# Moving the statistics of eight token tiles from VectorE to ScalarE, and splitting four operand sums in two

## The chip, the cores and the metric

One core of a Trainium2 chip. The metric is the device time of one execution in microseconds (us), the median of several runs. All matrix products are float32 values split into a high and a low part (fp32r), each product being three matmuls: high times high, high times low, low times high.

## The reference

```
x  = A_x                                    # 2048 tokens x 512
xn = (x - mean(x)) / sqrt(var(x) + 1e-5)    # per token
a  = xn @ dft_hid_re.T;  b = xn @ dft_hid_im.T
y  = dft_seq_re @ a - dft_seq_im @ b        # 2048 x 512
h  = gelu(xn @ w_gate) * (xn @ w_up)        # 512 -> 1792
out = x + y + h @ w_down
```

## The kernel before

x is held as 16 token tiles `xs[n]` of 128 tokens x 512 values. Each tile is normalised in place: mean and variance into the columns of one small tile `stats` (`ln_stats`: `bn_stats`, then `bn_aggr`, on VectorE), an approximate reciprocal root on ScalarE (`ln_root`), four small VectorE instructions that refine it (`ln_refine`), and one ScalarE activation with a scale and a bias column (`ln_affine`, L1304, "apply"). Then ScalarE rounds the tile to its high part (`split_hi`, L251) and VectorE subtracts to get the low part (`split_lo`, L256).

The sequence transform comes first, in four chunks of 512 columns. In chunk 0, token tiles 0 to 3 and 8 to 11 are multiplied plainly (the z matmuls, operands `pan`, `xa`, `xb`, `xf`). Tiles 4 to 7 (the set `J`) are paired with tiles 12 to 15, and each pair goes through a seven-product scheme of Strassen's kind (the m matmuls, operands `ps` and `xa`, `xf`, `xc`). In the later chunks all eight pairs do. A step of pass 0 of a pair multiplies products 0, 5, 6 and 4, a step of pass 1 products 1, 3 and 2; every product is 2 column halves x 3 matmuls. The x operands of products 4, 5, 6 and 2 are sums of quarters of the two tiles: `sum_of(k, 0..3)` forms four 128x256 sums on VectorE (L1364 to L1371); the sums for products 4 and 5 share one 128x512 tile, those for 6 and 2 another. `sum_hi` rounds such a tile on ScalarE in one instruction (`xch`), and `split_lo` gives its low part on VectorE (`xcl`). After the last pair of a pass the products are combined (L1440 to L1452) in the PSUM banks in which pass 1 goes on. The combined results of two chunks are multiplied with the hidden-dimension matrices (the y matmuls, operands z and d). After that come the two gated layers (a, b, c, dn matmuls).

The order of the instructions of chunks 0 and 1 is not written by hand. A planner (`Plan`) is given every operation with its engine, its cost in us, what it comes after and which buffers it uses. TensorE's order is fixed; the time at which TensorE would reach each product gives every other operation its due time. The planner then walks through time and gives each engine, among the operations that can start, the one that can start first, and among those the one due first; the list that results is the order of instructions on each engine. Nothing is reordered at run time. Loads go through SP's queue and stores to DRAM through POOL's, in the planner's order too. The engine names in the planner are p (TensorE), v (VectorE), a (ScalarE), s (SP), g (POOL). Costs that matter here: V5 .6, V2 .333, V1 .1 (VectorE: 512 columns, 256 columns, tiny), A5 .52, A2 .31 (ScalarE: 512 and 256 columns).

`group(ns)` enters the normalisation of one or two tiles; the groups are [2], [3], [8, 9], [10, 11] and the four pairs (4, 12), (5, 13), (6, 14), (7, 15). Tiles 0 and 1 are handled ahead of the planner.

Of the kernel before, what the change touches and what calls it, by code (L numbers as in the profile page):

```python
# [9 lines left out]
F32R = mybir.dt.float32r  # L10
BF16 = mybir.dt.bfloat16
AF = mybir.ActivationFunctionType
OP = mybir.AluOpType

P = 128
S = 2048
D = 512
# [8 lines left out]
HD = D // 2  # L26
HS = NS // 2
WARM = 9
WARM_END = 3
SLOTS = 109  # L30
J = (4, 5, 6, 7)
NP = NF
EPS = 1e-5

# [183 lines left out]
def fnet_geglu_kernel(ctx: ExitStack, tc: tile.TileContext, x, xt, cs, dh, wgu, wd, out):  # L218
# [7 lines left out]
    nc = tc.nc  # L226
# [8 lines left out]
    def slot(name, dtype=F32, shape=(P, D)):  # L235
        return mem.tile(list(shape), dtype, name=name, tag="mem")
# [13 lines left out]
    def split_hi(t, src, sign=1):  # L250
        nc.scalar.activation(t[0], src, AF.Copy, scale=float(sign))  # L251

    def split_lo(t, src, sign=1, engine=nc.vector):
        hi = t[0].bitcast(F32)
        if sign > 0:
            engine.tensor_sub(t[1], src, hi)  # L256
        else:
            engine.scalar_tensor_tensor(t[1], src, -1.0, hi, op0=OP.mult, op1=OP.subtract)
# [30 lines left out]
    stats = const.tile([P, 2, NS], F32, name="stats")  # L289
    ident = const.tile([P, P], F32, name="ident")  # L290
    eps = const.tile([P, 1], F32, name="eps")
# [10 lines left out]
    xs, ln, xn = {}, {}, {}  # L302
# [14 lines left out]
    def ln_stats(ns):  # L317

        ops = []
        for n in ns:  # L320
            parts = 1 if n else 2
            bn = small.tile([P, parts, 6], F32, name="bn")
            for h in range(parts):
                ops.append(lambda h=h, n=n, bn=bn, whole=parts == 1: nc.vector.bn_stats(
                    bn[:, h], xs[n] if whole else xs[n][:, h * HD:(h + 1) * HD]))
            ops.append(lambda n=n, bn=bn: nc.vector.bn_aggr(stats[:, :, n], bn))
        for i in range(2, len(ops) - 1, 2):
            if len(ns) > 1:
                ops[i - 1], ops[i] = ops[i], ops[i - 1]
        return ops  # L330

    def ln_root(ns):
        w = small.tile([P, 9], F32, name="w")
        var = stats[:, 1, span(ns)]
        nc.scalar.activation(w[:, :len(ns)], var, AF.Abs_reciprocal_sqrt, bias=eps)
        for n in ns:
            ln[n] = w

# [11 lines left out]
    def ln_refine(ns):  # L350
        k = len(ns)
        w = ln[ns[0]]
        r, t, b = (w[:, i * 3:i * 3 + k] for i in range(3))
        mean, var = (stats[:, i, span(ns)] for i in range(2))

        return [lambda a=a: nc.vector.scalar_tensor_tensor(*a[:4], op0=a[4], op1=OP.mult) for a in (
            (t, var, EPS, r, OP.add), (t, t, -0.5, r, OP.mult), (var, t, 1.5, r, OP.add), (b, mean, -1.0, var, OP.mult))]

    def ln_apply(ns, early=False):
        for i, n in enumerate(ns):  # L360
            src, kw = xs[n], dict(scale=stats[:, 1, n:n + 1], bias=ln[n][:, 6 + i:7 + i])
            his = []
            if n not in xn:
                if n < HS:
                    xn[n] = [hl_half(f"x{'ab'[h]}{n}") for h in range(1 if n in J else 2)]
                    his = [(xn[n][h][0], src[:, h * HD:(h + 1) * HD]) for h in range(len(xn[n]))]
# [17 lines left out]
    full = {}  # L384
    PL = [n for n in range(NS) if n % HS not in J]
    XO = PL + [n + h for n in J for h in (0, HS)]

# [97 lines left out]
    xc, xsum = {}, []  # L485
# [372 lines left out]
    def load_wd(q):  # L858

        if q < NP:  # L860
            wx["d", q] = [slot("wd", F32, (P, 2, HD)) for _ in range(2)]
# [11 lines left out]
    hs, hl, acc = {}, {}, {}  # L873
# [328 lines left out]
    warm = const.tile([P, CH], BF16, name="warm")  # L1202
# [42 lines left out]
        begin_products(k, slice(a, a + 1))  # L1245

    L = len(seq)
    V5, V2, V1, A5, A2, MB = .6, .333, .1, .52, .31, .262
    plan = Plan(dict(p=10.9, v=12.0, a=11.7, s=5.6, g=8.0), 18, SLOTS - 2, AHEAD)
    plan.dma, land = 12.8, 8.75  # L1250
# [18 lines left out]
    for n in range(2):  # L1269
        plan.done(("apply", n), 11.)  # L1270
        for h in range(2):
            plan.done(("xlo", n, h), 12.)
            plan.size["xn", n, h] = 1

    def group(ns):
        ops = ln_stats(ns)
        names, todo = [], [(n, f) for n in ns for f in ("bn", "ag")]
        if len(ns) > 1:
            for i in range(2, len(todo) - 1, 2):
                todo[i - 1], todo[i] = todo[i], todo[i - 1]  # L1280
        for (n, f), op in zip(todo, ops):
            plan.add((f, n), "v", .58 if f == "bn" else V1, op, after=[("x", n) if f == "bn" else ("bn", n)], uses=[("xs", n)])
        key = ns[0]
        plan.add(("root", key), "a", .2, lambda: ln_root(ns), after=[("ag", n) for n in ns])
        box = []

        def refine(i):
            if not box:
                box.extend(ln_refine(ns))
            box[i]()  # L1290
        for i in range(4):
            plan.add(("ref", key, i), "v", V1, lambda i=i: refine(i), after=[("ref", key, i - 1) if i else ("root", key)])
        for i, n in enumerate(ns):
            plan.add(("apply", n), "a", .72, lambda i=i, n=n: ln_affine(n, i), after=[("ref", key, 3)], uses=[("xs", n)])
            parts = 1 if n >= HS or n in J else 2
            for h in range(parts):
                wide = n >= HS
                plan.add(("xhi", n, h), "a", A5 if wide else A2, lambda n=n, h=h: x_hi(n, h), after=[("apply", n)],
                         uses=[("xs", n)], makes={("xn", n, h): 2 if wide else 1})
                plan.add(("xlo", n, h), "v", V5 if wide else V2, lambda n=n, h=h: x_lo(n, h), after=[("xhi", n, h)],  # L1300
                         uses=[("xs", n), ("xn", n, h)])
# [22 lines left out]
    def x_part(n, h):  # L1324
        return ("xlo", n, 0) if n >= HS else ("xlo", n, h)
# [16 lines left out]
    for k in range(2, L):  # L1342
        n, m = seq[k]
        for d in range(ND):
            xu = ("xn", n, d // 2 if n < HS else 0)
            plan.add(("pe", k, d), "p", 3 * MM, lambda k=k, d=d: plain_product(k, d), after=[("plo", k), x_part(n, d // 2)],
                     uses=[("ph", k)] + ([xu] if n < HS and d > 1 else []), holds=[("z", m, d)])
# [3 lines left out]
    st = {}  # L1351

    def sum_hi(k, r, t):
        hl = slot("xch", F32R, (P, 2, HD)), slot("xcl", F32R, (P, 2, HD))
        for i in range(2):
            xc[r[i], k] = hl[0][:, i], hl[1][:, i]
        split_hi(hl, t)
        st["hl", k, r[0]] = hl, t

    def sum_of(k, j):  # L1360
        u, v = xs[k], xs[k + HS]
        if j == 0:
            st[k, 0] = slot("xs", F32, (P, 2, HD))
            nc.vector.tensor_add(st[k, 0][:, 0], u[:, HD:], v[:, HD:])  # L1364
        elif j == 1:
            nc.vector.tensor_sub(st[k, 0][:, 1], st[k, 0][:, 0], u[:, :HD])
        elif j == 2:
            st[k, 1] = slot("xs", F32, (P, 2, HD))
            nc.vector.tensor_sub(st[k, 1][:, 0], u[:, :HD], u[:, HD:])
        else:  # L1370
            nc.vector.tensor_sub(st[k, 1][:, 1], v[:, :HD], st[k, 0][:, 1])  # L1371

    for k in range(HS):
        xu = [("xs", k), ("xs", k + HS)]
        both = [("apply", k), ("apply", k + HS)]
        for j, (after, tiles) in enumerate(((both, [("t", k, 0)]), ([("s", k, 0)], [("t", k, 0)]), (both, [("t", k, 1)]),
                                            ([("s", k, 1), ("s", k, 2)], [("t", k, 0), ("t", k, 1)]))):
            plan.add(("s", k, j), "v", V2, lambda k=k, j=j: sum_of(k, j), after=after, uses=xu + tiles[:None if j % 2 else 0],
                     makes={} if j % 2 else {tiles[0]: 1})
        for j, r in enumerate(((4, 5), (6, 2))):  # L1380
            plan.add(("shi", k, j), "a", A5, lambda k=k, j=j, r=r: sum_hi(k, r, st[k, j]), after=[("s", k, 2 * j + 1)],
                     uses=[("t", k, j)], makes={("xc", k, j): 2})
            plan.add(("slo", k, j), "v", V5, lambda k=k, r=r: split_lo(*st["hl", k, r[0]]), after=[("shi", k, j)],
                     uses=[("t", k, j), ("xc", k, j)])

    def operand(c, r, k):
        k = pair(c, k)
        xc[0, k], xc[1, k], xc[3, k] = xn[k][0], xn[k + HS][0], xn[k + HS][1]
        return xc[r, k]

    def operand_ready(c, r, k):
        k = pair(c, k)
        return {0: x_part(k, 0), 1: x_part(k + HS, 0), 3: x_part(k + HS, 1)}.get(r) or ("slo", k, 0 if r in (4, 5) else 1)

    def load_one(i, key):
        c, p, k = steps[i]
# [194 lines left out]
    for r, g in ((0, 0), (0, 1), (1, 0), (1, 1)):  # L1591
        plan.add(("y", r, g), "p", 12 * MM, lambda r=r, g=g: z_y(r, g), uses=[("do", r, g)] + [("z0", (r, g, e)) for e in range(2)],
                 after=[("dlo", r, g), *(("zlo", (r, g, e)) for e in range(2))],
                 banks=[("y", r, j) for j in range(2)] * (g == 0), holds=[("y", r, j) for j in range(2)])
        if g:
            plan.add(("yo", r), "a", 1.04, lambda r=r: y_copy(r), after=[("y", r, g), *([("res", 0, 0)] if r else ["st2"])],
                     makes={("po", r): 2}, holds=[("y", r, j) for j in range(2)])
# [9 lines left out]
    for g in range(2):  # L1607
        t = {(kb, oh): ("d2", g, kb, oh) for kb in range(2) for oh in range(2)}
# [9 lines left out]
    for kb in range(2):  # L1618
        for g in range(2):
            plan.add(("fz", kb, g), "s", .9, lambda kb=kb, g=g: fetch_z(0, kb, g), mb=2 * MB, makes={("zr", kb, g, e): 1 for e in range(2)},  # L1620
                     after=[("dzp", *KT[kb, g], e) for e in range(2)])
# [3 lines left out]
    for r in (4, 2, 6, 5, 3):  # L1625
        both = [("y", 1, r, j) for j in range(2)]
        for g in range(2):
            plan.add(("y", r, g), "p", 12 * MM, lambda r=r, g=g: z_y(r, g), uses=[("do", r, g)] + [("z", (r, g, e)) for e in range(2)],
                     after=[("dlo", r, g), *(("zlo", (r, g, e)) for e in range(2))], banks=both * (g == 0), holds=both)
# [3 lines left out]
    for j in range(4):  # L1633
        i = n1 + j
        c, p, k = steps[i]
# [4 lines left out]
        else:  # L1640
            for key in PANELS[p]:
                plan.add(("ld", i, key), "s", .45, lambda i=i, key=key: load_one(i, key), mb=MB, due=END + 12,
                         makes={("r", i, key): 1})
# [12 lines left out]
    for i, (c, p, k) in enumerate(steps):  # L1656
# [34 lines left out]
        else:  # L1691
            for n, (r, g) in enumerate((r, g) for r in (4, 2, 6, 5, 3)[:5 if c < NC - 1 else 3] for g in range(2)):
# [13 lines left out]
                if n in (2, 4) and c == NC - 1:  # L1706
                    t = n // 2 - 1
# [56 lines left out]
```

## Time and profile before

| | |
|---|---|
| median of 3 runs | 798.88 us (798.71 to 799.8) |
| profiled execution | 799.29 us, of which the profile's span is 797.2 us |
| TensorE busy | 792.6 us (99%) |
| VectorE busy | 722.3 us (91%) |
| ScalarE busy | 505.7 us (63%) |
| POOL busy | 157.2 us (20%) |
| DMA | 177.47 MB, mean 223 GB/s |

The page is of one execution. The span runs from the first to the last instruction; the profiled execution's own time is 2.09 us longer. In the views, PE is TensorE's matmuls, PEld its weight loads, DVE VectorE, ACT ScalarE, SPq the queue of SP. A row of a timeline has start and duration in us, engine, line, operation, output <- inputs with shapes, how many instructions it merges, and in brackets the idle time before it and what ended that. Durations of neighbours on an engine overlap, so the distance from start to start is what an instruction costs.

### The profile page before, as it was taken

To read this page: it belongs to the slowest core of one execution; us is meant where nothing else is said; L and a number is where in the kernel's file an instruction comes from. 1 tells how busy PE (TensorE), PEld (TensorE's weight loads), DVE (VectorE), ACT (ScalarE), POOL (GpSimd) and SP (SyncE) were. 2 spreads that over 40 slices of the span, in tenths; PEclk is the share of its full clock that TensorE was granted. 3 is DMA by queue.
4 is the path that set the end of the run, shared out by engine and by line. 5 is a ranking of instruction groups with operands and counts; after the bars stand their busy time and mean duration, and the time that the engine had idled before them with its cause. 6 is when DMAs were issued, how large, how long until landed. Compare 5 with 4: busy or idle time off the path is not lost.

```text
span 797.2 us, 11453 instructions
## 1 busy us (share of the span) xinstructions
PE 792.6 (99%) x3487; PEld 652.9 (82%) x3487; DVE 722.3 (91%) x1336; ACT 505.7 (63%) x952; POOL 157.2 (20%) x228
## 2 busy tenths in 40 slices
PE   9999999999999999999999999999999999999998
PEld 6888888888888888888888888888888888888886
DVE  7999999989999979899999998898878779989787
ACT  6786555556544555365658866866766677576564
POOL 0000510034211231000203422321222233121100
PEclk9999999999999999999999999999999999999999
DMA  9856898778999887778726987868965799887942
GB/s 334 314 183 199 303 345 256 248 252 256 373 359 331 327 282 290 261 263 302 189 65 139 210 160 167 191 111 212 264 125 97 123 237 152 174 209 139 250 109 106
DMA packets 90477, 177.47 MB, mean 223 GB/s; under 512 B 10832, under 2 KB 14448, under 8 KB 90224
## 3 DMA queue, kind: packets, MB, share of 16 engines
q1 hardware_dynamic: 65328, 118.27, 44.3%
q0 software_dynamic: 24800, 58.21, 34.4%
q8 instruction: 27, 0.44, 0.2%
q14 instruction: 34, 0.28, 0.1%
q10 hardware_dynamic: 288, 0.26, 0.1%
HBM read 114.29 MB, written 65.55 MB: 226 GB/s over the span
## 4 chain that ended last, share of the span: by engine, by line
PE 99%; DVE 0%; issue 0%; ACT 0%; DVEq 0%
PE m L267 33%; PE dn L267 17%; PE b L267 14%; PE c L267 10%; PE a L267 10%; PE y L267 9%; PE z L267 6%; PE warm L1207 1%; DVE dl L256 0%; DVE z411l L256 0%; ACT dh L251 0%; DVE ds L433 0%; DVE p L1002 0%; PE warm L1209 0%; DVE warm L1203 0%
## 5 line engine op out<-in xcount | busy, mean ns | idle before, releaser
L251 ACT ACTIVATE psh<-pan 128x512 fp32r<-128x512 f32 x196 | 112.3, 625 | 74.6 <-DVE pan L644 29.6
L256 DVE TENSOR_TENSOR psl<-pan,psh 128x512 fp32r<-128x512 f32 x196 | 125.9, 681 | 5.4 <-ACT psh L251 4.7
L923 POOL DMA_DIRECT2D partial<-part x94 | 81.0, 868 | 234.9 <-ACT part L922 200.9
L267 PE MATMUL m<-psh,xch 128*128 128x512 f32 x224 | 87.3, 390 | 0.0
L267 PE MATMUL m<-psl,xch 128*128 128x512 f32 x224 | 87.2, 389 | 0.0
L267 PE MATMUL m<-psh,xcl 128*128 128x512 f32 x224 | 87.2, 389 | 0.0
L922 ACT ACTIVATE part<-dn 128x512 f32<-128x512 f32 x94 | 55.4, 605 | 24.5 <-PE dn L267 22.2
L256 DVE TENSOR_TENSOR wl<-ws,wh 128x512 fp32r<-128x512 f32 x84 | 55.0, 683 | 0.3 <-ACT wh L251 0.2
L251 ACT ACTIVATE wh<-ws 128x512 fp32r<-128x512 f32 x84 | 49.6, 629 | 0.8 <-DMA xT_hl<-xT51h 0.7
L267 PEld LDWEIGHTS m<-psh,xch 128*128 128x128 f32 x224 | 42.0, 188 | 9.1 <-DVE m L1452 0.3
L267 PEld LDWEIGHTS m<-psh,xcl 128*128 128x128 f32 x224 | 42.0, 188 | 8.7
L267 PEld LDWEIGHTS m<-psl,xch 128*128 128x128 f32 x224 | 42.1, 188 | 8.7
L1147 ACT ACTIVATE w<-b 128x512 f32<-128x512 f32 x28 | 16.8, 599 | 47.0 <-PE b L267 46.9
L557 POOL DMA_DIRECT2D partial<-part x28 | 20.8, 787 | 106.3 <-ACT part L553 97.5
L1150 DVE TENSOR_TENSOR w<-c,w 128x512 f32<-128x512 f32 x28 | 19.3, 689 | 24.3 <-ACT w L1147 24.3
L256 DVE TENSOR_TENSOR htl<-s,hth 128x512 fp32r<-128x512 f32 x56 | 35.9, 684 | 4.2 <-ACT hth L251 4.1
L267 PE MATMUL m<-psh,xa 128*128 128x512 f32 x112 | 39.0, 389 | 0.0
L895 DVE TENSOR_TENSOR s<-s 128x512 f32<-128x512 f32 x56 | 37.4, 687 | 1.0
L639 DVE TENSOR_TENSOR pan<-pan 128x512 f32<-128x512 f32 x56 | 36.5, 678 | 0.0
L256 DVE TENSOR_TENSOR wl<-wx,wh 128x512 fp32r<-128x512 f32 x28 | 19.2, 686 | 16.2 <-ACT wh L251 16.2
L251 ACT ACTIVATE hth<-s 128x512 fp32r<-128x512 f32 x56 | 32.4, 642 | 1.0 <-DVE s L895 1.0
L267 PE MATMUL dn<-hl,wh 128*128 128x512 f32 x84 | 32.8, 390 | 0.0
(774 smaller groups left out, 2342.6 us busy)
## 6 DMA issues: line engine op xcount, KB each, us to landing
pan<-in_cs SPq DMA_DIRECT2D x156, 256.0 KB, 5.4
partial<-part POOLq DMA_DIRECT2D x122, 256.0 KB, 5.1
wx<-in_wgu SPq DMA_DIRECT2D x56, 256.0 KB, 4.9
t_park<-pan POOLq DMA_DIRECT2D x28, 256.0 KB, 5.0
pan<-t_park SPq DMA_DIRECT2D x28, 256.0 KB, 4.5
wd<-in_wd SPq DMA_DIRECT2D x28, 256.0 KB, 4.3
acc<-partial SPq DMA_DIRECT2D x28, 256.0 KB, 5.3
zr<-z_park SPq DMA_DIRECT2D x16, 256.0 KB, 4.0
```

The lines of the kernel that those rows point to most:

```text
L251: nc.scalar.activation(t[0], src, AF.Copy, scale=float(sign))
L256: engine.tensor_sub(t[1], src, hi)
L267: nc.tensor.matmul(ps, a[u][:, sl], b[v], start=first and r == 0, stop=last and r == 2, skip_group_check=resumed)
L557: nc.gpsimd.dma_start(partial[sp, r, j], ypart.pop((r, j)), **({} if r in (0, 5, 6) else {"accum_op": OP.add}))
L639: return [lambda: nc.vector.tensor_sub(t3, b22, b12), lambda: nc.vector.tensor_sub(t1, b12, b11), lambda: (nc.vector.tensor_sub(b22, b22, ...
L895: nc.vector.tensor_sub(t, u, v)
L922: nc.scalar.activation(t, ps[j], AF.Copy)
L923: nc.gpsimd.dma_start(partial[sp, r, j], t, accum_op=OP.add)
L1147: nc.scalar.activation(w, b, AF.Copy)
L1150: nc.vector.tensor_add(w, c, w)
L1207: nc.tensor.matmul(ps, warm[:, :P], warm, start=i == 0, stop=False)
```

## The change

For the tiles of the four pairs (4 to 7 and 12 to 15) the mean and the variance are computed by ScalarE: a Copy with scale 1/512 whose accumulated output is the mean, then a Square with scale -1 and the mean as its bias column, whose accumulated output is 512 times the variance. The elementwise output goes to the small `warm` tile and is not used. The root and the refinement take the factor 512 into account. In the planner the two are entered under the old names ("bn", n) and ("ag", n), now on engine a with costs 0.72 and 0.82.

For the same pairs the operand tile of products 6 and 2 is rounded and subtracted in two halves of 256 columns: high half and low half for product 6, then for product 2. The sum for product 2 comes after the high half of product 6. Product 2 waits for the second low half alone. `operand` sets the references to x operands one by one, for the product that uses them.

```diff
@@ -29,6 +29,7 @@
 WARM_END = 3
 SLOTS = 109
 J = (4, 5, 6, 7)
+AST = {n + h for n in J for h in (0, HS)}
 NP = NF
 EPS = 1e-5
 
@@ -332,7 +333,7 @@
     def ln_root(ns):
         w = small.tile([P, 9], F32, name="w")
         var = stats[:, 1, span(ns)]
-        nc.scalar.activation(w[:, :len(ns)], var, AF.Abs_reciprocal_sqrt, bias=eps)
+        nc.scalar.activation(w[:, :len(ns)], var, AF.Abs_reciprocal_sqrt, bias=eps, scale=1 / D if ns[0] in AST else 1.0)
         for n in ns:
             ln[n] = w
 
@@ -353,8 +354,9 @@
         r, t, b = (w[:, i * 3:i * 3 + k] for i in range(3))
         mean, var = (stats[:, i, span(ns)] for i in range(2))
 
+        m = D if ns[0] in AST else 1
         return [lambda a=a: nc.vector.scalar_tensor_tensor(*a[:4], op0=a[4], op1=OP.mult) for a in (
-            (t, var, EPS, r, OP.add), (t, t, -0.5, r, OP.mult), (var, t, 1.5, r, OP.add), (b, mean, -1.0, var, OP.mult))]
+            (t, var, EPS * m, r, OP.add), (t, t, -0.5 / m, r, OP.mult), (var, t, 1.5, r, OP.add), (b, mean, -1.0, var, OP.mult))]
 
     def ln_apply(ns, early=False):
         for i, n in enumerate(ns):
@@ -1245,6 +1247,7 @@
         begin_products(k, slice(a, a + 1))
 
     L = len(seq)
+    ASUM = .72
     V5, V2, V1, A5, A2, MB = .6, .333, .1, .52, .31, .262
     plan = Plan(dict(p=10.9, v=12.0, a=11.7, s=5.6, g=8.0), 18, SLOTS - 2, AHEAD)
     plan.dma, land = 12.8, 8.75
@@ -1272,14 +1275,24 @@
             plan.done(("xlo", n, h), 12.)
             plan.size["xn", n, h] = 1
 
+    def act_mean(n):
+        nc.scalar.activation(warm, xs[n], AF.Copy, scale=1 / D, accum_out=stats[:, 0, n:n + 1])
+
+    def act_var(n):
+        nc.scalar.activation(warm, xs[n], AF.Square, scale=-1.0, bias=stats[:, 0, n:n + 1], accum_out=stats[:, 1, n:n + 1])
+
     def group(ns):
-        ops = ln_stats(ns)
-        names, todo = [], [(n, f) for n in ns for f in ("bn", "ag")]
-        if len(ns) > 1:
-            for i in range(2, len(todo) - 1, 2):
-                todo[i - 1], todo[i] = todo[i], todo[i - 1]
-        for (n, f), op in zip(todo, ops):
-            plan.add((f, n), "v", .58 if f == "bn" else V1, op, after=[("x", n) if f == "bn" else ("bn", n)], uses=[("xs", n)])
+        if ns[0] in AST:
+            for n in ns:
+                plan.add(("bn", n), "a", ASUM, lambda n=n: act_mean(n), after=[("x", n)], uses=[("xs", n)])
+                plan.add(("ag", n), "a", ASUM + .1, lambda n=n: act_var(n), after=[("bn", n)], uses=[("xs", n)])
+        else:
+            todo, ops = [(n, f) for n in ns for f in ("bn", "ag")], ln_stats(ns)
+            if len(ns) > 1:
+                for i in range(2, len(todo) - 1, 2):
+                    todo[i - 1], todo[i] = todo[i], todo[i - 1]
+            for (n, f), op in zip(todo, ops):
+                plan.add((f, n), "v", .58 if f == "bn" else V1, op, after=[("x", n) if f == "bn" else ("bn", n)], uses=[("xs", n)])
         key = ns[0]
         plan.add(("root", key), "a", .2, lambda: ln_root(ns), after=[("ag", n) for n in ns])
         box = []
@@ -1357,6 +1370,13 @@
         split_hi(hl, t)
         st["hl", k, r[0]] = hl, t
 
+    def half_hi(k, i):
+        if i == 0:
+            hl = slot("xch", F32R, (P, 2, HD)), slot("xcl", F32R, (P, 2, HD))
+            for e in range(2):
+                xc[(6, 2)[e], k] = hl[0][:, e], hl[1][:, e]
+        split_hi(xc[(6, 2)[i], k], st[k, 1][:, i])
+
     def sum_of(k, j):
         u, v = xs[k], xs[k + HS]
         if j == 0:
@@ -1374,10 +1394,17 @@
         xu = [("xs", k), ("xs", k + HS)]
         both = [("apply", k), ("apply", k + HS)]
         for j, (after, tiles) in enumerate(((both, [("t", k, 0)]), ([("s", k, 0)], [("t", k, 0)]), (both, [("t", k, 1)]),
-                                            ([("s", k, 1), ("s", k, 2)], [("t", k, 0), ("t", k, 1)]))):
+                                            ([("s", k, 1), ("s", k, 2), *[("shi", k, 1)] * (k in J)], [("t", k, 0), ("t", k, 1)]))):
             plan.add(("s", k, j), "v", V2, lambda k=k, j=j: sum_of(k, j), after=after, uses=xu + tiles[:None if j % 2 else 0],
                      makes={} if j % 2 else {tiles[0]: 1})
         for j, r in enumerate(((4, 5), (6, 2))):
+            if j and k in J:
+                for i in range(2):
+                    plan.add(("shi", k, 1 + i), "a", A2, lambda k=k, i=i: half_hi(k, i), after=[("s", k, 2 + i)],
+                             uses=[("t", k, 1), ("xc", k, 1)] if i else [("t", k, 1)], makes={} if i else {("xc", k, 1): 2})
+                    plan.add(("slo", k, 1 + i), "v", V2, lambda k=k, i=i: split_lo(xc[(6, 2)[i], k], st[k, 1][:, i]),
+                             after=[("shi", k, 1 + i)], uses=[("t", k, 1), ("xc", k, 1)])
+                continue
             plan.add(("shi", k, j), "a", A5, lambda k=k, j=j, r=r: sum_hi(k, r, st[k, j]), after=[("s", k, 2 * j + 1)],
                      uses=[("t", k, j)], makes={("xc", k, j): 2})
             plan.add(("slo", k, j), "v", V5, lambda k=k, r=r: split_lo(*st["hl", k, r[0]]), after=[("shi", k, j)],
@@ -1385,12 +1412,14 @@
 
     def operand(c, r, k):
         k = pair(c, k)
-        xc[0, k], xc[1, k], xc[3, k] = xn[k][0], xn[k + HS][0], xn[k + HS][1]
+        for q, n, h in ((0, k, 0), (1, k + HS, 0), (3, k + HS, 1)):
+            if q == r:
+                xc[r, k] = xn[n][h]
         return xc[r, k]
 
     def operand_ready(c, r, k):
         k = pair(c, k)
-        return {0: x_part(k, 0), 1: x_part(k + HS, 0), 3: x_part(k + HS, 1)}.get(r) or ("slo", k, 0 if r in (4, 5) else 1)
+        return {0: x_part(k, 0), 1: x_part(k + HS, 0), 3: x_part(k + HS, 1)}.get(r) or ("slo", k, 0 if r in (4, 5) else 1 + (r == 2 and k in J))
 
     def load_one(i, key):
         c, p, k = steps[i]
```

## Prediction

> **What bounds the kernel now.** I read the page first, for the share of each engine, then TensorE's timeline for its cadence, then the stretches of 10 us, because the edited work lies between 20 and 100 us.
>
> ```profile
> span 797.2 us, 11453 instructions
> PE 792.6 (99%) x3487; PEld 652.9 (82%) x3487; DVE 722.3 (91%) x1336; ACT 505.7 (63%) x952; POOL 157.2 (20%) x228
> ```
>
> A busy PE is not yet a PE at its peak, so the starts of single matmuls decide. These are the first z matmuls after the slow start, the first m matmul of each sequence chunk, and the widest gap between them:
>
> ```profile
> 8.01 0.62 PE L267 MATMUL z<-panh,xa 128*128 128x512 f32 x2
> ...
> 49.73 0.39 PE L267 MATMUL m<-psh,xa 128*128 128x512 f32 x1
> ...
> 98.84 0.39 PE L267 MATMUL m<-psh,xa 128*128 128x512 f32 x1
> ...
> 177.93 0.40 PE L267 MATMUL y<-z410h,dh 128*128 128x512 f32 x1
> 178.46 0.50 PE L267 MATMUL y<-z410h,dl 128*128 128x512 f32 x1
> ...
> 202.99 0.39 PE L267 MATMUL m<-psh,xa 128*128 128x512 f32 x1
> ```
>
> From 8.01 to 49.73 us the code issues 184 z matmuls (16 panels x 4 blocks x 3 terms, less the 8 before 8.01): 41.72 / 184 = 0.2267 us each, with no gap. From 49.73 to 98.84 it issues 4 pairs x 42 + 4 y blocks x 12 = 216: 48.98 us at that rate, and 49.11 passed, so 0.13 is lost. From 98.84 to 202.99 it issues 8 x 42 + 10 x 12 = 456: 103.39 us against 104.15, so 0.76 is lost, 0.30 of it in the one gap at 178 (0.53 between starts). **All that TensorE could win in the part that the planner orders is 0.13 + 0.76 = 0.9 us, 0.11% of the time.** The number of matmuls doesn't change.
>
> ```profile
> 20.00:30.00 10.00, 10.00 (x45) 8.26 (x45) 10.00 (x30) 5.53 (x12) 0.00 (x0) 1.00 1.04 379
> 30.00:40.00 10.00, 10.00 (x46) 8.27 (x45) 10.00 (x26) 8.84 (x18) 0.72 (x1) 1.00 0.70 248
> 40.00:50.00 10.00, 10.00 (x46) 8.29 (x45) 9.81 (x27) 9.00 (x18) 0.56 (x1) 1.00 0.53 177
> 50.00:60.00 10.00, 10.00 (x46) 8.29 (x45) 10.00 (x25) 8.55 (x16) 1.05 (x2) 1.00 0.56 184
> 60.00:70.00 10.00, 10.00 (x46) 8.29 (x45) 9.81 (x19) 8.70 (x17) 0.03 (x1) 1.00 0.67 210
> 70.00:80.00 10.00, 10.00 (x46) 8.29 (x45) 10.00 (x18) 5.11 (x9) 0.00 (x0) 1.00 0.55 187
> ```
>
> The columns after the stretch's length are PE, PEld, DVE, ACT and POOL, busy time each. VectorE is full, but it runs ahead of TensorE: a full engine that nobody waits for. ScalarE has 4.47 + 1.16 + 1.00 + 1.45 + 1.30 = 9.4 us free from 20 to 70 us, and 4.9 in the ten after. The granted clock is 1.00 throughout.
>
> **VectorE's side of the change.**
>
> ```profile
> 51.04 1.28 DVE L324 BATCH_NORM_STATS2 bn<-x 128x6 f32<-128x512 f32 x2
> 52.23 0.41 DVE L1364 TENSOR_TENSOR xs<-x,x 128x256 f32<-128x256 f32 x1
> 52.56 0.42 DVE L256 TENSOR_TENSOR xa<-x,xa 128x256 fp32r<-128x256 f32 x1
> ...
> 56.31 0.24 DVE L326 BATCH_NORM_AGGREGATE stats<-bn 128x2 f32<-128x6 f32 x2
> 56.47 0.66 DVE L639 TENSOR_TENSOR pan<-pan 128x512 f32<-128x512 f32 x1
> ```
>
> What an operation costs its engine is the distance to the next start. Two statistics take 52.23 - 51.04 = 1.19, two aggregates 0.16; eight tiles take 8 x (0.60 + 0.08) = 5.4 us, which go. The low parts of the sums (6, 2) become two halves: 2 x 0.33 for 0.60, so 4 x 0.06 = 0.3 us more. VectorE wins 5.1 us, all before about 60 us. Nothing waits for VectorE there, so the gain on the path is zero by itself. It can only shrink the 0.9 us.
>
> **ScalarE's side.**
>
> ```profile
> 14.62 0.81 ACT L1304 ACTIVATE x<-x,w,stats 128x512 f32<-128x512 f32 x1
> 15.46 0.42 ACT L251 ACTIVATE xa<-x 128x256 fp32r<-128x256 f32 x1
> 15.79 0.40 ACT L251 ACTIVATE xb<-x 128x256 fp32r<-128x256 f32 x1
> 16.09 0.28 ACT L335 ACTIVATE w<-stats,eps 128x1 f32<-128x1 f32 x1
> 16.28 2.70 ACT L251 ACTIVATE panh<-pan 128x512 fp32r<-128x512 f32 x5
> ...
> 23.45 1.52 ACT L1304 ACTIVATE x<-x,w,stats 128x512 f32<-128x512 f32 x2 [1.41 <-DVE w L356]
> 24.88 0.62 ACT L251 ACTIVATE xf8h<-x 128x512 fp32r<-128x512 f32 x1
> ```
>
> Plain copies of 128x512 take (2.70 - 0.62) / 4 = 0.52 each, those with two column operands 1.43 / 2 = 0.71, one column operand by halving 0.62. A half copy takes 0.31 to 0.33. No row shows an accumulating activation. The bounds for what reading out the sum adds: nothing (the sum comes along), or a small activation of its own, whose nearest row is the root's, 0.19 to its successor, at most its whole 0.28. The second activation of a tile reads the mean that the first has just written. The nearest row for such a pair is 14.62 and 15.46: the copy of what the same engine had just written starts 0.84 after, 0.13 more than 0.71. So one tile costs between 0.52 + 0.62 = 1.14 and 0.52 + 0.71 + 2 x 0.28 + 0.13 = 1.92. I take 0.52 + 0.62 + 2 x 0.19 = 1.52, since the root is the only row as narrow as a read-out; the planner's own costs (0.72 and 0.82) say 1.54. Eight tiles: 12.2 us (9.1 to 15.4). The four divided high parts add 4 x 0.1 = 0.4. ScalarE's load rises by 12.6 us (9.5 to 15.8).
>
> The Trainium skill, VectorE: DVE Perf Modes, § The DRAIN you can't avoid, says that a same-engine read after a write needs a semaphore, and names a ScalarE accumulator output among what is read stale without one; the 0.13 us above agrees with a wait there, and no run here shows it for an accumulator. By it, a mean and a variance that stand back to back pay it every time; the sum by it would be about 1 us more on ScalarE, inside the range above.
>
> **Does it fit?** Against 12.6 us stand 9.4 free us and work that ran early only because ScalarE was free:
>
> ```profile
> L251 ACT ACTIVATE psh<-pan 128x512 fp32r<-128x512 f32 x19 | 11.0, 620 | 1.2 <-DVE w L356 0.6 <-DVE pan L639 0.5
> ...
> L251 ACT ACTIVATE dh<-d 128x512 fp32r<-128x512 f32 x3 | 1.8, 615 | 0.0
> ...
> L251 ACT ACTIVATE xf12h<-x 128x512 fp32r<-128x512 f32 x1 | 0.6, 617 | 0.0
> L251 ACT ACTIVATE xf13h<-x 128x512 fp32r<-128x512 f32 x1 | 0.6, 617 | 0.0
> ```
>
> These are groups between 20 and 67 us. Three of the 19 panels belong to the second pass (4 steps x 4 operands are 16), the three d parts to the y blocks (from 49.73 + 168 x 0.2267 = 87.8 us), and the tiles 12 to 15 are wanted from 49.73 + 96 x 0.2267 = 71.5 us on: 10 x 0.52 = 5.2 us. The halves of product 2 (4 x 0.31 = 1.2) are wanted only in the second pass too. That is 15.8 us of room for 12.6, with 3 to spare; at the dear end, none.
>
> ```profile
> 31.92 2.38 ACT L251 ACTIVATE psh<-pan 128x512 fp32r<-128x512 f32 x4
> ...
> 26.74 0.91 SPq L309 DMA_DIRECT2D x<-in_x  x2
> ...
> DMA to landing us min/median/max: 2.8/5.4/6.4
> ```
>
> The x tiles are there in time: the last two are issued from 26.74 to 27.65, and the slowest landing took 6.4, so all lie in SBUF by about 34. The 4.47 us free from 20 to 30, such as the 1.41 before 23.45, can take statistics of the earlier tiles.
>
> SP loses no instruction. The statistics' chain is about 0.9 us longer (1.54 + waits against 0.68), so x tiles become due that much earlier and may pass a panel or two in SP's queue, 0.45 us each. The panels beside them are those of the m steps: their first high parts run at 31.92, their first matmul at 49.73, and these 18 us hide it; without them it would cost about 1 us. POOL's transfers stand where they stood.
>
> Queued behind the new activations on ScalarE are the high parts, without which VectorE's low parts and then TensorE wait. The slack at the last pair, by its latest operand, is that of the rows below: xcl done at 65.77, used at 69.22, so 3.4 us. At the end of the first pass it is much less:
>
> ```profile
> 65.08 0.69 DVE L256 TENSOR_TENSOR xcl<-xs,xch 128x512 fp32r<-128x512 f32 x1
> ...
> 72.64 1.28 DVE L1452 TENSOR_TENSOR m<-m,p 128x512 f32<-128x512 f32 x2
> ...
> 69.22 0.39 PE L267 MATMUL m<-psh,xcl 128*128 128x512 f32 x1
> ...
> 74.21 0.39 PE L267 MATMUL m<-psh,xch 128*128 128x512 f32 x1
> ...
> 66.93 1.28 ACT L1440 ACTIVATE p<-m 128x512 f32<-128x512 f32 x2 [0.99 <-PE m L267]
> ```
>
> The chain copy of product 0, sums on VectorE, product 2 ends at 73.92 and is used at 74.21: 0.29 us. Its first link now finds ScalarE idle for 0.99 us before.
>
> The change also adds a wait: the fourth sum of a pair (VectorE) stands behind the high half of the third (ScalarE, 0.40 us in the row at 15.79). Behind it on VectorE are panel sums and low parts. With 5.1 us won there, four such waits of up to 0.7 us (a copy on ScalarE to be finished first) are covered; without that cover they would be 2.8 us of VectorE's lead, which is 3.4 us at the last pair. In turn the root no longer waits for VectorE's aggregate.
>
> **Sum.** Profiled execution 799.29 us (span 797.2 and 2.09 around it). TensorE's cadence unchanged; of the 0.9 us I take 0.2 as won, since the gap at 178 is a chain of VectorE and ScalarE in turn that a lighter VectorE shortens only in part. 799.1, and 0.41 less on the scale of the median (798.88): **798.7 us**. If all gaps closed: 798.0.
>
> **Rivals.** *ScalarE late* (slower). The order is fixed beforehand with 1.54 us a tile. If a tile really costs 1.92, ScalarE is 8 x 0.38 = 3.0 us behind its plan when product 0 ends at 67 us; less 0.29, TensorE stands 2.7 us: 801.6. It decides once the lateness exceeds what idle is left ahead of 67 us plus 0.3. For it: 9.4 us idle shrink to almost none. Against it: the planner moves 5 to 6 us of other work out, and its other costs match the rows (0.52, 0.60, 0.33). Chance 0.17, from 800.5 to 801.6.
>
> *Table switches* (slower). Square is new beside the root and the copies:
>
> ```profile
> L335 ACT ACT_TABLE_LOAD x1 | 1.3, 1283 | 1.2 <-PEq L1757 1.2
> ```
>
> One load serves root, Copy and Identity now. If Square lay in another table, four roots between squares would need up to eight loads, 8 x 1.28 = 10.3 us; with 3 us to spare ScalarE is 7 us late, 805.6. Chance 0.03. The Trainium skill, ScalarE: Activation LUTs, § Table sets: the hidden batching unit, names relu, copy, identity and abs as in every set and does not name square; by it the loads would be open, and no run here shows them yet.
>
> *TensorE wins more than its gaps* (faster). I see no place: 0.9 us is under the 0.2% (1.6 us) that a measurement of this kernel can tell from no change. Chance 0.04, for what lies outside the trace.
>
> *The relief isn't used*: VectorE, waiting for a later ScalarE, gives the 5.1 us back as idle time. That lands in the forecast, at 798.9.
>
> **Numbers.** Forecast 0.76 (798.0 to 800.4), which is "within 0.2%". Slower by over 0.2%: 0.17 + 0.03 = 0.20; faster 0.04. The range runs from 798.0 to 801.6; outside lie the table switches, the faster case and a tail of the first rival.
>
> **What would show it.** Eight bn and ag pairs gone from VectorE, 16 new activations on ScalarE between 21 and 56 us with spacing near 0.72 and 0.82; VectorE with idle time from 20 to 70 where it had almost none; ScalarE over 9.5 of 10 there; the distance 8.01 to 49.73 unchanged. I am wrong if TensorE's starts between 49.7 and 76 us show gaps with ScalarE as the releaser, or if a second table load stands among the statistics.

## The result and the profile after

The changed kernel takes 798.03 us (median of 22 runs, 797.39 to 799.13) against 799.12 us (22 runs of the kernel before beside it, 798.63 to 799.81). The ratio is 0.9987, 95% interval 0.9981 to 0.9993: 1.09 us less, between 0.6 and 1.5. The forecast was "within 0.2%", 0.2 us less, in a range from 798.0 to 801.6: the time lies at the lower edge of the range, where the prediction put it "if all gaps closed".

The page of the changed kernel, first lines:

```profile
span 796.4 us, 11491 instructions
PE 791.9 (99%) x3487; PEld 653.0 (82%) x3487; DVE 717.6 (90%) x1324; ACT 515.7 (65%) x988; POOL 156.9 (20%) x228
```

The same number of matmuls, 4.7 us less of VectorE, 10 us more of ScalarE, 0.8 us less of span (the profiled execution took 798.22 us, the one before 799.29). The last matmul of the kernel before, then TensorE's timeline of the changed kernel at the places that matter:

```profile
793.64 0.28 PE L267 MATMUL dn<-htl,w 128*128 128x256 f32 x1
```

```profile
49.56 0.39 PE L268 MATMUL m<-psh,xa 128*128 128x512 f32 x1
...
144.72 0.39 PE L268 MATMUL m<-psh,xf12l 128*128 128x512 f32 x1
145.22 0.50 PE L268 MATMUL m<-psh,xch 128*128 128x512 f32 x1
...
178.03 0.39 PE L268 MATMUL y<-z410h,dh 128*128 128x512 f32 x1
178.26 0.39 PE L268 MATMUL y<-z410h,dl 128*128 128x512 f32 x1
...
792.91 0.28 PE L268 MATMUL dn<-htl,w 128*128 128x256 f32 x1
```

The two starts at 178, 0.53 us apart before, are 0.23 apart now. At 145 a gap of 0.27 us (0.50 less 0.227) stands, wider than before (0.11). The last matmul ends the stretch that I use from here on: from the first m to the last matmul's start, 792.91 - 49.56 = 743.35 us, where the kernel before has 793.64 - 49.73 = 743.91.

The stretches of the kernel before, then those of the changed one (columns: length, PE, PEld, DVE, ACT, POOL, granted clock, DMA):

```profile
20.00:70.00 50.00, 50.00 (x222) 41.40 (x222) 49.62 (x123) 40.62 (x77) 2.36 (x4) 1.00 0.70 240
140.00:180.00 40.00, 39.87 (x176) 32.43 (x175) 37.70 (x63) 21.76 (x39) 7.59 (x14) 1.00 0.76 251
```

```profile
20.00:70.00 50.00, 50.00 (x223) 41.38 (x222) 49.91 (x124) 49.39 (x110) 2.36 (x4) 1.00 0.62 216
70.00:80.00 10.00, 10.00 (x46) 8.29 (x45) 10.00 (x19) 8.57 (x18) 0.00 (x0) 1.00 0.30 97
140.00:180.00 40.00, 39.89 (x176) 32.59 (x175) 33.73 (x56) 18.52 (x33) 7.57 (x14) 1.00 0.78 263
```

ScalarE is full from 20 to 70 us, and TensorE doesn't notice: from the first m to 145 us its profile has no gap of 0.1 us. VectorE is as full there as before: it used what was taken off it to run ahead with other work, and the idle time comes out late, 6.3 us instead of 2.3 from 140 to 180.

ScalarE's timeline shows what the new operations cost:

```profile
21.97 0.62 ACT L1279 ACTIVATE warm<-x 128x512 bf16<-128x512 f32 x1
22.50 0.19 ACT L1279 ACTIVATION_READ_ACCUMULATOR warm<-x 128x1 f32 x1
22.72 0.63 ACT L1279 ACTIVATE warm<-x 128x512 bf16<-128x512 f32 x1
23.25 0.19 ACT L1279 ACTIVATION_READ_ACCUMULATOR warm<-x 128x1 f32 x1
23.34 0.62 ACT L252 ACTIVATE panh<-pan 128x512 fp32r<-128x512 f32 x1
...
45.85 0.71 ACT L1282 ACTIVATE warm<-x,stats 128x512 bf16<-128x512 f32 x1
46.46 0.19 ACT L1282 ACTIVATION_READ_ACCUMULATOR warm<-x,stats 128x1 f32 x1
46.69 0.72 ACT L1282 ACTIVATE warm<-x,stats 128x512 bf16<-128x512 f32 x1
47.32 0.19 ACT L1282 ACTIVATION_READ_ACCUMULATOR warm<-x,stats 128x1 f32 x1
47.41 0.40 ACT L252 ACTIVATE xch<-xs 128x256 fp32r<-128x256 f32 x1
```

Reading the sum out is an instruction of its own. From its start to the start of the next instruction it takes 0.09 us ahead of a copy and 0.22 ahead of another accumulating activation. A mean costs 0.62 or 0.75, a variance 0.72 or 0.84; the eight tiles come to 11.6 us, 1.45 a tile.

### The profile page after: what moved, and what is told of

The parts are those of the page before. It is cut to its first block, busy times and chain, and to the rows that moved or that the text cites. A ratio compares the mean times of both kernels' runs of the same rounds, so it can differ in the third digit from the quotient of the medians.

```text
span 796.4 us, 11491 instructions
## 1 busy us (share of the span) xinstructions
PE 791.9 (99%) x3487; PEld 653.0 (82%) x3487; DVE 717.6 (90%) x1324; ACT 515.7 (65%) x988; POOL 156.9 (20%) x228
## 4 chain that ended last, share of the span: by engine, by line
PE 99%; DMA 1%; DVE 0%; issue 0%; DVEq 0%
PE m L268 33%; PE dn L268 17%; PE b L268 14%; PE c L268 10%; PE y L268 10%; PE a L268 10%; PE z L268 6%; DMA xd<-in_xt 1%; PE warm L1209 1%; DVE c L1479 0%; DVE m L1481 0%; DVE p L1004 0%; PE warm L1211 0%; DVE warm L1205 0%; PE st L1614 0%
## 5 line engine op out<-in xcount | busy, mean ns | idle before, releaser
L268 PE MATMUL dn<-hl,wh 128*128 128x512 f32 x84 | 32.8, 390 | 0.0
```

What stands on the lines that cost most here:

```text
L268: nc.tensor.matmul(ps, a[u][:, sl], b[v], start=first and r == 0, stop=last and r == 2, skip_group_check=resumed)
```

## The experiments

Three theories. A: the lighter VectorE closes TensorE's gaps. B: the split, which lets product 2 come later, does. C: every new order of the planner puts such gaps in other places, whatever it lightens. The table has them all; "heavy" kernels keep the eight tiles' statistics on VectorE, "light" ones don't (few_stats: only 16 of 512 columns). Column 3 is the stretch from the first m to the last matmul in each profile, column 4 the gaps of TensorE in it of 0.1 us and more (excess over the cadence of 0.2267, follow-up gaps added).

| kernel | ratio to before (95%) | first m to last matmul | gaps, at us: size |
|---|---|---|---|
| before, two profiles (heavy) | 1 | 743.91, 744.03 | 145: 0.1; 178: 0.4; 200: 0.1; 204: 0.2 in the second; 393: 0.2 |
| before_order (heavy) | 0.9998 (0.9989 to 1.0007) | 744.04 | 145: 1.2 |
| before_order2 (heavy) | 0.9999 (0.9990 to 1.0007) | 743.81 | 145: 0.9 |
| before_order3 (heavy) | 1.0040 (1.0027 to 1.0053) | 747.96 | 73 to 75: 0.3; 139 to 148: 3.1; 207: 0.4; 251: 0.9 |
| split_only (heavy) | 1.0011 (1.0001 to 1.0020) | 745.29 | 145: 0.7; 247 to 251: 1.6 |
| the change, two profiles (light) | 0.9987 (0.9981 to 0.9993) | 743.35, 743.02 | 145: 0.4 and 0.1 |
| after_order (light) | 1.0003 (0.9994 to 1.0012) | 744.77 | 145: 0.9; 178: 1.0 |
| after_order2 (light) | 0.9993 (0.9984 to 1.0002) | 743.28 | 178: 0.4 |
| after_order3 (light) | 0.9991 (0.9982 to 0.9999) | 743.32 | 178: 0.4 |
| stats_only (light) | 0.9989 (0.9980 to 0.9998) | 742.92 | none |
| few_stats (light) | 0.9994 (0.9985 to 1.0003) | 743.36 | 203: 0.4 |
| mean_twice | 1.0050 (1.0036 to 1.0063) | 748.20 | 67 to 78: 3.8; 147 to 150: 1.0; 209: 0.3 |

### One part alone

```diff
 # stats_only, against the change
-            if j and k in J:
+            if False:
 # ... (two more lines: the fourth sum does not wait for the high half, and product 2 waits for the undivided sum again)
```

> The statistics of the eight tiles on ScalarE as in the change, the sums of products 6 and 2 in one part as before. Theory A (the lighter VectorE closes the gaps of TensorE at 178 and 200 us, the split adds nothing): 0.5 to 1.1 us under before, as the whole change (-1.09); no gap over 0.1 us between 175 and 203 us. Theory B (the split, which asks for product 2 later, is what helps): within 0.3 us of before, the gap at 178 still there. Theory C (any new order of the planner shuffles such gaps, whatever it lightens): some change between -0.5 and +1, with gaps of 0.1 to 0.5 at new places.

```diff
 # split_only, against the change
-AST = {n + h for n in J for h in (0, HS)}
+AST = set()
```

> The sums of products 6 and 2 in two parts, all statistics on VectorE as before. Theory A: within 0.3 us of before, or slower by it, since VectorE has 0.3 us more to do; the gap near 178 us remains. Theory B: 0.5 us or more under before. Theory C: between -0.5 and +1, gaps elsewhere.

The statistics alone bring what the whole change brings: 0.9 us less (0.2 to 1.6), and no gap of 0.1 us:

```profile
177.42 0.39 PE L268 MATMUL y<-z410h,dh 128*128 128x512 f32 x1
177.64 0.39 PE L268 MATMUL y<-z410h,dl 128*128 128x512 f32 x1
...
792.30 0.28 PE L268 MATMUL dn<-htl,w 128*128 128x256 f32 x1
```

The split alone is 0.9 us slower (0.1 to 1.6). B is out. But A had said within 0.3, with the gap at 178 in place, and that gap is gone; others stand at 145 and here, far from the edited work:

```profile
247.21 0.39 PE L268 MATMUL m<-psh,xf12l 128*128 128x512 f32 x1
248.62 0.51 PE L268 MATMUL m<-psh,xf12h 128*128 128x512 f32 x1 [1.03 <-ACT m L709]
```

Followed back on VectorE, the lateness begins where VectorE waits for a panel load in chunk 2:

```profile
224.48 1.29 DVE L641 TENSOR_TENSOR pan<-pan 128x512 f32<-128x512 f32 x2 [3.25 <-DMA pan<-in_cs]
```

That VectorE then runs some 2 us behind the kernel before (the sum into product 0, L703 here and L701 there, starts at 246.06 instead of 243.88) is shown; that this wait alone makes the gap was argued from the rows, and why the load came late was not tried.

### ScalarE's load taken away, and added to

```diff
 # few_stats, against the change
+nc.vector.bn_stats(few[n][:, 0], xs[n][:, :16])      # on "v", cost V1, in place of act_mean
+nc.vector.bn_aggr(stats[:, :, n], few[n])            # on "v", cost V1, in place of act_var
 # ... (the factor 512 goes out of the root and the refinement)
```

> The split as in the change, but the statistics of the eight tiles are taken by VectorE from 16 of their 512 columns (left out: the other 496), so VectorE is nearly as light as in the change and ScalarE has no load of the statistics at all. Theory A: the same as the change within 0.4 us (0.6 to 1.4 under before), because ScalarE's added 12.6 us are hidden. If ScalarE's load costs the change something: more than 0.5 us faster than the change. Theory C: anything within 1 us of before.

```diff
 # mean_twice, against the change
     def act_mean(n):
+        nc.scalar.activation(warm, xs[n], AF.Copy, scale=1 / D, accum_out=stats[:, 0, n:n + 1])
         nc.scalar.activation(warm, xs[n], AF.Copy, scale=1 / D, accum_out=stats[:, 0, n:n + 1])
```

> The change with every mean computed twice on ScalarE, the second time unknown to the planner: 8 x 0.71 = 5.7 us more there before 57 us, in the order of the change. By the prediction's first rival (lateness at 67 us less what idle is left and 0.3 us of slack is a stall of TensorE; ScalarE has 0.6 us idle from 20 to 70 us in the profile of the change): TensorE stands 4.5 to 5 us between 60 and 76 us, 3.4 to 4 us over before. If the slack of the operands (3 to 6 us) hides it: under 1 us over the change.

Without any load on ScalarE the stretch is 743.36 us, the change's own 743.35 and 743.02: the added 12 us of ScalarE are hidden, as A had it and C allowed. (few_stats also has its own order, so the equal stretch alone would not show it; the change's profile, without a gap before 145 us, does.) The time is 0.5 us under before (0.2 over to 1.2 under), less than A asked for; a new gap of 0.4 us stands at 203.

Twice the mean is the first rival of the prediction, made to happen. By the rows the second means add 6.0 us. ScalarE's copy of product 0 starts at 71.13 instead of 66.76, 4.4 us late, and TensorE stands three times: once for a high part of x, for whose kind the prediction counted 3.4 us of slack, and twice in the chain of copies and sums that it named as the tight place:

```profile
67.02 0.51 PE L268 MATMUL m<-psh,xa 128*128 128x512 f32 x1 [0.96 <-ACT xa L252]
...
75.63 0.50 PE L268 MATMUL m<-psh,xf12h 128*128 128x512 f32 x1 [0.96 <-ACT m L1477]
...
77.86 0.50 PE L268 MATMUL m<-psh,xch 128*128 128x512 f32 x1 [0.57 <-DVE m L1482]
```

ScalarE's row for the copy, and the stretch from 20 to 70 us, in which the late ScalarE leaves VectorE idle for 4.5 us:

```profile
71.13 0.58 ACT L1470 ACTIVATE p<-m 128x512 f32<-128x512 f32 x1
```

```profile
20.00:70.00 50.00, 48.98 (x215) 39.61 (x214) 45.50 (x115) 49.52 (x115) 2.36 (x4) 1.00 0.62 214
```

The stalls between 65 and 78 us sum to 3.8 us, where 4.5 to 5 were expected; the time is 4.0 us over before (2.9 to 5.0), where 3.4 to 4 were expected. The stall is smaller than expected because the chain has more slack than the 0.3 us taken from the prediction. Its last row merges two sums of 0.69 us, and product 2 starts behind the first of them, as mean_twice shows (77.12 + 0.69 = 77.81, used at 77.86):

```profile
77.12 0.69 DVE L1482 TENSOR_TENSOR m<-m,p 128x512 f32<-128x512 f32 x1
```

In the change that first sum ends at 72.64 + 0.69 = 73.33 and is used at 74.04, 0.7 us later:

```profile
72.64 1.29 DVE L1481 TENSOR_TENSOR m<-m,p 128x512 f32<-128x512 f32 x2
...
74.04 0.39 PE L268 MATMUL m<-psh,xch 128*128 128x512 f32 x1
```

The sum comes 4.5 us late (77.12 instead of 72.64); less 0.7 that is the 3.8 us. So of 6.0 us more on ScalarE 3.8 come out at TensorE within 20 us: the change has some 2.2 us of room there, by this one point.

### The same work in other orders

> The kernel before once more, for a second profile of the same program: TensorE's gaps that belong to the order (145, 178, 200 us) stand again at the same places; those at its first z matmuls (5 to 8 us) and at 393 us may differ, and are then no effect of the change. Theory C has no word on this.

> The changed kernel once more: the gap at 145 us of 0.3 to 0.4 stands again, none at 178 and 200; the distance from the first m matmul (49.6) to the first a matmul (382) is 332.5 within 0.2, where the kernel before has 332.8.

Second profiles tell the order from chance. In the kernel before, 145, 178, 200 and 393 stand again (393 too, which I had left to chance); the z stage takes 44.33 us in one and 43.86 in the other, so 0.5 us of a run's time, in gaps before 12 us, belongs to no order. In the change the gap at 145 was 0.1 instead of the expected 0.3 to 0.4, and the first a matmul came 332.1 us after the first m, where 332.3 to 332.7 was expected: a gap of one order varies by some 0.3 us too.

```diff
 # before_order: the planner's costs only
-    V5, V2, V1, A5, A2, MB = .6, .333, .1, .52, .31, .262
+    V5, V2, V1, A5, A2, MB = .61, .339, .1, .52, .31, .262
 # after_order, against the change
-    ASUM = .72
+    ASUM = .8
```

> The kernel before, with the planner's costs of VectorE's 512 and 256 column operations raised by under 2% (0.60 to 0.61, 0.333 to 0.339), so that only the order of the same instructions changes. Theory A (the lighter VectorE closes the gaps): within 0.4 us of before, gaps at 145, 178 or 200 in sum as before. Theory C (any new order shuffles them): a change of 0.5 us or more either way, gaps at other places.

> The changed kernel with the planner's cost of a statistics activation at 0.80 in place of 0.72 (and 0.90 for 0.82): the same instructions in another order. Theory A: 0.6 to 1.4 us under before, like the change. Theory C: anywhere from 1 us under to 1 us over before, gaps at new places.

Neither theory holds whole. The kernel before keeps its time (0.9 us under to 0.6 over), as A said, but its gaps at 178 and 200 are gone and one of 1.1 us stands at 145, as C said. And the changed work in another order loses all that it had won, against A:

```profile
145.63 0.50 PE L268 MATMUL m<-psh,xch 128*128 128x512 f32 x1 [0.60 <-DVE m L1481]
...
178.44 0.49 PE L268 MATMUL y<-z410h,dh 128*128 128x512 f32 x1
179.58 0.50 PE L268 MATMUL y<-z410h,dl 128*128 128x512 f32 x1 [0.65 <-DVE dl L257]
```

The gap at 178 is 0.9 us here, with VectorE busy 32.8 of 40 us around it. So the last question was whether a light VectorE is worth something in the mean of orders (A2):

```diff
 # before_order2: V5, V2 = .59, .328      before_order3: .62, .344
 # after_order2:  ASUM = .68              after_order3: V5, V2 = .61, .339 in the change
```

> The kernel before in another order: VectorE's costs in the planner lowered to 0.59 and 0.328. Theory C, which the first two reorderings favour (the order alone decides, the lighter VectorE has no value of its own): from 1 us under to 1 us over before; the stretch from the first m to the last matmul anywhere from 743.0 to 744.8 us (743.9 and 744.0 in the kernel before). Theory A2 (the lighter VectorE is worth some 0.5 us in the mean of several orders): 744.0 or more.

> The kernel before in a third order: VectorE's costs raised to 0.62 and 0.344. Theory C: the stretch from the first m to the last matmul from 743.0 to 744.8 us, within 1 us of before. Theory A2: 744.0 us or more.

> The changed kernel in another order: cost of a statistics activation 0.68 in place of 0.72. Theory C: the stretch from the first m to the last matmul from 743.0 to 744.8 us, within 1 us of before. Theory A2: under 743.6 us (743.35 and 743.0 in the changed kernel, 744.8 with 0.80).

> The changed kernel with VectorE's costs in the planner at 0.61 and 0.339, those that moved the kernel before from gaps at 178 and 200 us to one of 1.1 us at 145. Theory C: 743.0 to 744.8 us from the first m to the last matmul. Theory A2: under 743.6 us.

Both light ones came under 743.6, as A2 said. Of the heavy ones, 743.81 missed A2's bound by 0.2, and 747.96 lies beyond what C allowed. Over all: five light kernels lie between 742.9 and 743.4 us and one at 744.8; the five heavy ones lie between 743.8 and 748.0. No heavy order reached what the usual light order gives, some 0.6 us better; a bad order undoes that twice over. With six and five orders this is a tendency, not a law.

For the gap at 178 the rows settle it. TensorE waits there for `dl`, which comes from a sum `ds` on VectorE, its high part on ScalarE and the subtraction of that on VectorE. In the kernel before (heavy) and in after_order2 (light) `ds` stands behind the low part z411l in VectorE's order:

```profile
172.64 1.37 DVE L1530 TENSOR_TENSOR zr<-c,zr 128x512 f32<-128x512 f32 x2 [1.70 <-ACT c L1511]
...
175.73 0.68 DVE L256 TENSOR_TENSOR z411l<-zr,z411h 128x512 fp32r<-128x512 f32 x1
176.33 0.68 DVE L433 TENSOR_TENSOR ds<-d 128x512 f32<-128x512 f32 x1
...
177.71 0.69 DVE L256 TENSOR_TENSOR dl<-ds,dh 128x512 fp32r<-128x512 f32 x1
```

```profile
172.35 1.37 DVE L1559 TENSOR_TENSOR zr<-c,zr 128x512 f32<-128x512 f32 x2 [6.04 <-ACT c L1540]
...
176.03 0.69 DVE L435 TENSOR_TENSOR ds<-d 128x512 f32<-128x512 f32 x1
...
177.41 0.69 DVE L257 TENSOR_TENSOR dl<-ds,dh 128x512 fp32r<-128x512 f32 x1
```

In the change (light) and in before_order2 (heavy) it stands ahead of both low parts:

```profile
172.80 1.32 DVE L1559 TENSOR_TENSOR zr<-c,zr 128x512 f32<-128x512 f32 x2 [5.39 <-ACT c L1540]
...
175.28 0.68 DVE L435 TENSOR_TENSOR ds<-d 128x512 f32<-128x512 f32 x1
175.88 0.68 DVE L257 TENSOR_TENSOR z410l<-zr,z410h 128x512 fp32r<-128x512 f32 x1
...
177.08 0.68 DVE L257 TENSOR_TENSOR dl<-ds,dh 128x512 fp32r<-128x512 f32 x1
```

```profile
173.04 1.31 DVE L1530 TENSOR_TENSOR zr<-c,zr 128x512 f32<-128x512 f32 x2 [2.96 <-ACT c L1511]
...
175.52 0.68 DVE L433 TENSOR_TENSOR ds<-d 128x512 f32<-128x512 f32 x1
...
177.33 0.68 DVE L256 TENSOR_TENSOR dl<-ds,dh 128x512 fp32r<-128x512 f32 x1
```

The heavy and the light kernel of the first order have the gap, 0.4 us in both; those of the second have none. In all four VectorE had just been idle (1.7 to 6.0 us), waiting for the copy `c`, so there was no load left to take off it. This gap goes with the order and not with the load. What tendency there is can be seen at 145: the sums that TensorE waits for there (L1452, L1481 in the change) start 94.7 to 98.1 us after the first m in the heavy kernels and 93.7 to 95.4 in the light ones. The two overlap.

## Why the prediction was right, and where its size was off

**TensorE's cadence as the bound** held. From 49.7 to 203 us the prediction counted 0.89 us lost; stats_only, with no gap of 0.1 us, shows that this much could be had (743.91 to 742.92). That bound is why nothing near 1% was possible. Of the 0.13 us before 98.84, some 0.09 is no gap to win: it stands in every kernel (at 90 us in the kernel before), where TensorE has one small matmul more that the count left out (`st<-ident,stats`). The bound was a little narrow: it ended at 203 us, and the gap of 0.2 us at 393, in both profiles of the kernel before and in no other kernel's, went too. The matmul (393.53) waits there for a product on VectorE (L1150, 392.79 + 0.68 = 393.47); why VectorE is late there in this order alone stays open.

**The term that was mis-sized** is the share of the 0.9 us that is won. I took 0.2, because the gap at 178 is a chain of VectorE and ScalarE in turn. Measured, the change's two profiles are 0.6 and 1.0 us under the mean of the two before (743.97), and the medians 1.09 (interval from 0.6, so not surely more than the 0.9). The reason was half right: in after_order, after_order2 and after_order3 that gap does outlive a light VectorE. In the change and in stats_only it does not, and that is the order, not a shorter chain: before_order2 has the same order with a heavy VectorE and no gap either. Four of the five heavy orders have no gap at 178. So the lighter VectorE did not earn the 0.4 us there; that this order came with the change was luck, and so is the part of the 1.09 us that hangs on it.

**VectorE's side**: 5.1 us less was predicted, busy time fell by 4.7. That it would show as idle time from 20 to 70 us was wrong: VectorE was busy 49.9 of 50, and the idle time came after 80: the relieved engine ran ahead first.

**ScalarE's side**: 12.2 us was predicted for eight tiles, from the root's 0.19 as a stand-in for the read-out; measured 11.6. The pair of mean and variance never stood back to back in the profile, so no run shows the wait of 0.13 us between them, nor what the Trainium skill, VectorE: DVE Perf Modes, § The DRAIN you can't avoid, says of such a read. ScalarE full at 9.9 of 10 from 20 to 70 was right.

**Rivals.** ScalarE late: not in the change, but mean_twice shows the mechanism as described, and its price within 1 us. Its 0.29 us of slack was a misreading: it was taken to the end of a row of two sums (73.92), but product 2 starts behind the first, so in the kernel before it was 74.21 - 73.33 = 0.9. Table switches: none. The groups of the changed kernel's first 380 us have one load, that at the start:

```profile
L336 ACT ACT_TABLE_LOAD x1 | 1.3, 1283 | 1.2 <-PEq L1786 1.2
```

So Square lies with the root and the copies here, which the Trainium skill, ScalarE: Activation LUTs, § Table sets: the hidden batching unit, left open.

That TensorE wins more than its gaps is not shown. The 1.6 us that the prediction took as the least difference to be told is too much, since with 22 runs of each kernel the interval is 0.9 us wide.

## What to carry to other kernels

When the bounding engine runs at its cadence, as TensorE here, its gaps summed over the stretch that an edit can reach are all that the edit can win; find that sum first, and expect some part of it. Where a planner orders the instructions, an edit changes the work and the order at once: perturb a cost by 2 to 3% with the work unchanged, on both sides, before crediting the work (0.62 for VectorE's measured 0.60 cost the kernel before 3.1 us), and compare stretches between two matmuls rather than whole times, which scatter more. Then compare the order of the instructions ahead of each gap: where a heavy and a light kernel with the same order have the same gap, the load is not its cause. A merged row ends with its last instruction, but the next engine may wait for its first alone.

## What the runs showed of the hardware beyond that

An accumulating activation is two instructions in the profile: the activation, at the cost of a plain one (0.53 us to the next start), and a read of the accumulator of 0.19 us that costs 0.09 us ahead of a plain activation and 0.22 ahead of another accumulating one. And the z stage of one and the same program differs by 0.5 us between two executions (44.33 and 43.86 us), in gaps before 12 us, about as much as the difference between usual orders studied here.
